# Softmax reciprocals taken on four sums instead of 256 copies of them, and a new hand-ordered issue table

## The chip, the cores and the metric

The kernel runs on one core of one Trainium2 chip. The metric is the device time of one execution in microseconds. Three runs of the kernel before gave 616.99, 620.66 and 622.17 us; their median is 620.66 us. The engines are PE (matrix multiply; PEld is its weight load), DVE (vector), ACT (activations), POOL (GpSimd) and SP, which here only issues DMAs.

## What is computed

Three stages, one behind the other, on 1152 tokens of width 512:

```python
# attention, B=2, H=8, S=576, D=64
scores = q @ k.T / 8 + bias          # bias: a 32-wide MLP of log1p|i-j| / log1p(max(i,1)), per head
attn = exp(scores - max)
attn = attn / (attn.sum(-1) + 1e-9)  # the sums and their reciprocals
x = (attn @ v) as [1152, 512]
# MLP, 512 -> 2048 -> 512
h = x @ w_in;  g = h * tanh(softplus(h));  y = g @ w_out
# mixture of 8 experts, 512 -> 1024 -> 512, one expert per token, at most 288 tokens each
e = argmax(y @ w_gate);  p = softmax(y @ w_gate)[e]
out = p * (relu(y @ w1[e]) @ w2[e])  # rows over the capacity stay zero
```

## The kernel before

**Tiling.** Tokens go in five tiles `it` = 0 to 4 of 256, 256, 256, 256 and 128 rows (the last holds the end of both batches). For each tile the program writes a bias block to memory (`bias_block`, L453) and reads it back by head, does attention head pair by head pair (`pair`, L523; `recips`, L577; `pv_pair`, L598; `x_out`, L615), then the MLP in eight steps (`mlp_a`, L711; `mlp_b`, L738), and writes `y` to the scratch tensor `yscr` and chooses each row's expert (`y_out`, L812; `rank_of`, L881). In the first 160 us the raw weights `wi` and `wo` are also turned into pairs of 16-bit numbers (`conv_row`, L632), with DVE, ACT and POOL sharing the passes over 128x1024 blocks.

**The reciprocals.** For a tile and a head pair the exponentials (L552) leave their row sums in a small tile `rsm`, 128x4 (128x2 in the last tile). `recips` adds 1e-9 (through helper line L279) and takes reciprocals (L588) with an input that reads each sum 64 times, so that one instruction makes a 128x256 tile (128x128 in the last). PE transposes it (L593), ACT or DVE copies it back from PSUM (L596), and `x_out` multiplies the attention output by it (L626, L629). There are 20 of these: 16 wide, 4 half as wide.

**Order.** Nothing is scheduled at run time. `op(...)` collects the operations of the first two stages with estimated times, and `emit` (L232) issues them in the order of a table of numbers, `ORDER`: a number divided by 8 is the operation, and the remainder chooses one of its `alt` forms, that is, the engine. Each engine runs its own queue in that order and waits, at the head of its queue, for what an instruction needs. The estimated times written in the `op` calls and the dependences of an operation that issues nothing change no instruction; only the table does. Which slot of a ring a buffer gets follows from the order too.

**The end of the second stage.** The last tile's `y` (128 rows) goes to `yscr` by two writes of 64 rows (L847, L848). SP's queue also holds the loads of the first expert's weights (`load1`, L1001, and `load2`, L1004, 512 KB each). The choice of experts ends in `gid0` (L991), the row numbers of the first expert's tokens; it needs sums `acc` that L962 adds up on POOL or DVE. Then POOL gathers those rows from `yscr` (L1163), which needs `gid0` and every write to `yscr`. SP reads the table of slots (L1156). The experts (L1176 to L1273) are written in program order, outside the table; four of the eight are run with these inputs.

```python
o.ways[c % 8][2]()          # emit: the chosen form of operation c // 8
gather(0)                   # POOL: three indirect DMAs, xg <- yscr by gid0
```

Of the kernel before, what the change touches and what calls it, by code (L numbers as in the profile page):

```python
# [22 lines left out]
P = 128  # L23
# [239 lines left out]
def tile_kernel(ctx: ExitStack, tc: tile.TileContext, a: dict, cap: int):  # L263
# [313 lines left out]
    def recips(it, ct):  # L577
# [6 lines left out]
        def f():  # L584
            x = sm.t[:, 4:4 + 2 * n]
            ts(dve, x, sm.t[:, 0:2 * n], 1e-9, ALU.add)
            (s0, n0), (s1, _) = x.ap
            dve.reciprocal(wide().rearrange("p (c i r) -> p c i r", c=n, i=2), bass.AP(x.tensor, x.offset, [[s0, n0], [s1, n], [s1 * n, 2], [0, 64]]))  # L588
# [789 lines left out]
```

## Time and profile before

| | before |
|---|---|
| median of three runs | 620.66 us (616.99 to 622.17) |
| profiled execution, its own time | 622.87 us |
| its span, first to last instruction | 621.1 us |
| busy: PE, DVE, ACT, POOL | 513.6, 439.9, 353.9, 129.9 us |
| mean granted TensorE clock | 0.92 of full speed |

The profiled execution's own time is 1.8 us above its span, and 2.2 us above the median. Busy shares are means over stages with different limits: weight conversion and the first attention tiles up to about 160 us, a long middle of attention and MLP up to 480 us, the change to the experts up to 510 us, then the experts. A clock of 1.00 is 2.4 GHz, 0.50 is 1.2 GHz; means between them are mixtures of the two.

### The profile page before, as it was taken

Reading aid. Unit: us, or ns where it says so; the run is one execution under the profiler, and the core shown is the slowest. Engines: PE = TensorE matmul, PEld = TensorE weight load, DVE = VectorE, ACT = ScalarE, POOL = GpSimd, SP = SyncE. Lnnn points to the kernel's source line nnn. Section 1 sums busy time; section 2 is a strip of 40 time slices with the busy share of each in tenths; the row PEclk is TensorE's granted clock in tenths of the full one; section 3 lists DMA queues with packets and bytes.
Section 4 is the critical chain, followed back from the end, with each engine's and each line's share of the span. In section 5 each row is a group of like instructions: output and inputs, shape, how many; then the busy total and the mean of one; then the engine's idle time right before and its main releaser. Section 6 shows DMA issues by size and latency. Waiting matters only on the chain.

```text
span 621.1 us, 11278 instructions
## 1 busy us (share of the span) xinstructions
PE 513.6 (83%) x4212; PEld 356.2 (57%) x4212; DVE 439.9 (71%) x966; ACT 353.9 (57%) x699; POOL 129.9 (21%) x152
## 2 busy tenths in 40 slices
PE   2562787999989989989899988979798539999975
PEld 0110345676567554445676654658556529999963
DVE  6998999899857849777866857346767725546462
ACT  7899888786645856765634653324544204545451
POOL 3502313012001120210011043115114410123212
PEclk9656689799999989999999999979899859999998
DMA  7987566510101225213443010213002245182810
GB/s 305 351 312 265 213 215 221 164 51 1 39 22 54 90 79 173 91 59 134 143 129 94 1 47 0 62 58 120 2 1 69 51 159 203 39 298 57 319 43 27
DMA packets 28468, 73.92 MB, mean 119 GB/s; under 512 B 5126, under 2 KB 5254, under 8 KB 26352
## 3 DMA queue, kind: packets, MB, share of 16 engines
q1 hardware_dynamic: 26704, 68.95, 32.6%
q0 software_dynamic: 1696, 4.11, 2.1%
q8 instruction: 36, 0.59, 0.4%
q14 instruction: 32, 0.26, 0.1%
HBM read 55.67 MB, written 17.61 MB: 118 GB/s over the span
## 4 chain that ended last, share of the span: by engine, by line
PE 52%; DVE 24%; DMA 9%; issue 7%; ACT 4%; POOL 2%; SPq 1%; POOLq 0%; DVEq 0%; ACTq 0%
PE pb L753 10%; PE pb L720 7%; PE pb L612 6%; DMA xg<-yscr,gid 5%; PE ps L720 5%; PE ps L534 4%; DVE rw L282 3%; PE py L1209 3%; PE ph L1186 3%; DVE ra L551 2%; PE pb L560 2%; PE pt L1186 2%; DVE ra L282 2%; DVE ra L588 2%; PE pb L472 2%
## 5 line engine op out<-in xcount | busy, mean ns | idle before, releaser
L720 PEld LDWEIGHTS <-WIt 128*128 128x128 f16 x960 | 86.9, 100 | 23.2 <-issue 12.0
L720 PE MATMUL pb<-PX,WIt 128*128 128x256 f16 (+1 forms) x672 | 74.4, 267 | 1.3 <-DVE ra L282 1.3
L753 PE MATMUL pb<-WOt,ra 128*128 128x512 f16 x276 | 67.4, 390 | 2.1 <-DVE ra L282 2.1
L552 ACT ACTIVATE ra<-ra,rm 128x576 f32<-128x576 f32 x58 | 44.8, 774 | 24.7 <-DVE rm L551 23.2
L460 ACT ACTIVATE ra<-AT,b1c,stab 128x528 f32<-128x528 f32 (+14 forms) x79 | 56.0, 749 | 2.3 <-DVE rm L551 1.3
L472 PE MATMUL pb<-ra,w2s 128*32 128x512 f32 (+17 forms) x248 | 39.3, 620 | 18.8 <-ACT ra L460 8.3
L534 PE MATMUL ps<-AT,rq 64*128 64x512 f32 (+1 forms) x160 | 44.4, 687 | 4.1 <-DVE rm L551 2.9
L753 PEld LDWEIGHTS <-ra 128*128 128x128 f16 x276 | 27.0, 100 | 32.5 <-issue 7.0
L612 PE MATMUL pb<-ra,AT 128*64 128x128 f32 (+1 forms) x660 | 40.7, 273 | 1.6 <-DVE ra L563 1.6
L551 DVE CUSTOM_DVE_ANT_0 ra<-ps,ra 128x576 f32<-128x576 f32 x48 | 34.9, 748 | 8.9 <-PE ps L537 8.7
L1209 PE MATMUL py<-HH,W 128*128 128x288 f32 x288 | 40.4, 298 | 0.0
L1008 DVE TENSOR_TENSOR W<-AT,W 128x1024 fp32r<-128x1024 f32 x28 | 33.7, 1223 | 9.2 <-ACT W L1007 8.4
L279 POOL TENSOR_SCALAR rw<-rw 128x1024 uint32<-128x1024 uint32 (+1 forms) x17 | 23.4, 1377 | 78.0 <-DMA rw<-wo 26.3
L1209 PEld LDWEIGHTS py<-HH,W 128*128 128x128 f32 x288 | 38.8, 188 | 0.0
L720 PE MATMUL ps<-PX,WIt 128*128 128x256 f16 (+1 forms) x288 | 32.5, 266 | 7.6 <-DVE ra L282 3.5
L612 PEld LDWEIGHTS pb<-ra,AT 128*64 128x64 f32 x660 | 34.1, 142 | 6.9 <-issue 4.3
L282 DVE SCALAR_TENSOR_TENSOR rw<-rw 128x1024 int32<-128x1024 int32 (+1 forms) x25 | 32.4, 1295 | 1.1 <-POOL rw L279 1.0
L560 PE MATMUL pb<-ident,ra 128*128 128x128 f32 x183 | 30.2, 290 | 2.2 <-ACT ra L552 1.9
L472 PEld LDWEIGHTS pb<-ra,w2s 128*32 128x32 f32 x248 | 8.1, 128 | 37.4 <-ACT ra L460 16.0
L1007 ACT ACTIVATE W<-AT 128x1024 fp32r<-128x1024 f32 x28 | 29.0, 1054 | 0.0
L537 PEld LDWEIGHTS ps<-AT,rq 128*128 128x128 f32 (+1 forms) x80 | 10.9, 186 | 30.4 <-issue 30.4
L563 ACT COPY ra<-pb 128x384 f32<-128x384 f32 x45 | 20.3, 475 | 13.9 <-PE pb L560 13.9
(386 smaller groups left out, 1114.5 us busy)
## 6 DMA issues: line engine op xcount, KB each, us to landing
AT<-m SPq DMA_DIRECT2D x32, 512.0 KB, 5.3
bscr<-rbe SPq DMA_DIRECT2D x36, 295.5 KB, 3.6
rw<-wo SPq DMA_DIRECT2D x8, 1024.0 KB, 5.3
ra<-bscr SPq DMA_DIRECT2D x24, 288.0 KB, 3.7
WOt<-wi SPq DMA_DIRECT2D x4, 1024.0 KB, 12.5
rw<-wi SPq DMA_DIRECT2D x4, 1024.0 KB, 15.6
AT<-k SPq DMA_DIRECT2D x4, 576.0 KB, 6.6
rw<-bscr SPq DMA_DIRECT2D x8, 288.0 KB, 3.1
```

The costliest lines, as they stand in the source:

```text
L282: (eng or dve).scalar_tensor_tensor(out=out, in0=in0, scalar=s, in1=in1, op0=op0, op1=op1)
L460: on_act = lambda h_=h_, g=g: act.activation(h_.t[:, 0:dn], T[:, 0:dn], AF.Relu, scale=stab[:, g:g + 1], bias=b1c)
L472: pe.matmul(ps.t[32 * c:32 * c + 32, 0:d1 - d0], w2s, hs[c].t[:, d0:d1], start=True, stop=True)
L534: pe.matmul(s_.t[r, 1024 * i:1024 * i + 512], q_.t[hs, c], kraw[hs, k0 + 576 * bb:k0 + 576 * bb + 512], start=True, stop=True)
L551: op("DVE", c_dve(S), lambda i=i, own=own, m_=m_, b_=b_: dve.tensor_tensor_reduce(out=own(), in0=blk(s_.t[:, 960 * i:960 * i + S]), in1=bl ...
L552: op("ACT", c_act(S, 2), lambda i=i, m_=m_, col=col: act.activation(t_.t[:, S * i:S * i + S], t_.t[:, S * i:S * i + S], AF.Exp, bias=m_.t[ ...
L560: pe.transpose(pa.t[:, P * j:P * j + P], t_.t[:, 384 * n + P * j:384 * n + P * j + P], ident)
L612: pe.matmul(ov[64 * i:64 * i + 64, ct % 2, w * bb:w * bb + w], v_, t_.t[:, at + c0:at + c0 + w], start=n == 0, stop=n == 4)
L720: pe.matmul(ps.t[:, n * f_:n * f_ + n], WI[:, wv, ct, P * ft:P * ft + P], xt.t[:, xv, ct, 0:n], start=i == 0, stop=i == 11)
L753: pe.matmul(y_.t, gv()[:, g2, c:c + P], WO[:, wv, ft], **kw)
L1008: dve.tensor_tensor(out=dst[:, 1], in0=src, in1=dst[:, 0].bitcast(F32), op=ALU.subtract)
L1209: pe.matmul(ps[:, 0:SL], W2[:, wv, ft, P * dt:P * dt + P], HH[:, hv, ft], start=ft == 0 and i == 0, stop=ft == 7 and i == 2)
```

## The change

Three things are changed. `recips` takes the reciprocal of the 128x4 sums in place and then copies the four numbers over the 256 columns, as an operation of its own that the table may give to DVE or ACT. Four estimates that the table was made from are different numbers, and the operation that stands for the gather and issues nothing now names `yscr`. And the table itself is new throughout.

```diff
 ORDER = [
-    160, 304, 1192, 120, 136, 168, 144, 152, 192, 312, 112, 176, 200, 1200, 128, 1209, 0, 8, 208, 88, 16, 760, 1216,
...
+    160, 416, 14552, 112, 152, 304, 120, 14560, 312, 168, 136, 144, 176, 200, 128, 1192, 1200, 0, 8, 208, 530, 768,
...
-        op("PE", 1150, f, bytes=0.5, r=[q_, ("k", ct), "kt"], w=[s_], p=["Kfree"], mode=2)
+        op("PE", 1277, f, bytes=0.5, r=[q_, ("k", ct), "kt"], w=[s_], p=["Kfree"], mode=2)
...
-        def f():
-            x = sm.t[:, 4:4 + 2 * n]
-            ts(dve, x, sm.t[:, 0:2 * n], 1e-9, ALU.add)
-            (s0, n0), (s1, _) = x.ap
-            dve.reciprocal(wide().rearrange("p (c i r) -> p c i r", c=n, i=2), bass.AP(x.tensor, x.offset, [[s0, n0], [s1, n], [s1 * n, 2], [0, 64]]))
-        op("DVE", 210 + 133 * n, f, w=[sm, b_], lk=1)
+        x = lambda: sm.t[:, 4:4 + 2 * n]
+
+        def small():
+            ts(dve, x(), sm.t[:, 0:2 * n], 1e-9, ALU.add)
+            dve.reciprocal(x(), x())
+        op("DVE", 210, small, w=[sm])
+
+        def ends_():
+            (s0, n0), (s1, _) = x().ap
+            return wide().rearrange("p (c i r) -> p c i r", c=n, i=2), bass.AP(x().tensor, x().offset, [[s0, n0], [s1, n], [s1 * n, 2], [0, 64]])
+        op("DVE", c_dve(P * n), lambda: dve.tensor_copy(*ends_()), r=[sm], w=[b_], alt=[("ACT", c_act(P * n), lambda: act.copy(*ends_()))])
...
-        op("PE", 1095 if it < NIT else 1300, f, ...
+        op("PE", 1142 if it < NIT else 1300, f, ...
...
-    op("POOL", 3700, lambda: None, r=["gid0"], w=["xg"])
+    op("POOL", 1000, lambda: None, r=["gid0", "yscr"], w=["xg"])
```

In the changed kernel lines behind the table stand one further down, and those behind `recips` six further down (L588 is L589, the new copy is L595, L1163 is L1169).

**SP, end of the second stage.** `AT<-m` are the loads of the first expert's weights, `yscr` the writes of y, `tb` the read of the slot table. Before:

```order
L303 DMA yscr<-rw_110 128x512
L1004 ISA
L1004 DMA AT<-m 128x2x512
L303 DMA out<-ra_112 128x512
L303 DMA yscr<-rw_110 64x512
L1004 ISA
L1004 DMA AT<-m 128x2x512
...
L303 DMA yscr<-rw_110 64x512
L303 DMA yscr<-ra_114 128x512
L1156 ISA
L1156 DMA tb_4581<-tbl 96x3x2
```

Now:

```order
L1010 DMA AT<-m 128x2x512
L304 DMA yscr<-ra_117 128x512
L304 DMA yscr<-ra_114 128x512
L1010 ISA
L1010 DMA AT<-m 128x2x512
L304 DMA yscr<-rw_110 128x512
L304 DMA out<-ra_118 128x512
L304 DMA yscr<-ra_118 64x512 x2
L1162 ISA
L1162 DMA tb_4601<-tbl 96x3x2
```

Before, the first 64 rows of the last tile stand ahead of two weight loads, and the other 64 rows and a block of 128 rows behind them. Now all weight loads stand ahead of the last tile's rows, and the two writes of 64 rows are the last ones, together.

**POOL, the same place.** `tbl` is the scatter into the slot table, `acc` the sums for `gid0`, `xg` the gather. Before:

```order
L915 DMA tbl_81<-pk6_165,rm5_130 2304x2
L962 TENSOR_TENSOR acc1_176<-acc1_176,rw2_110 128x288
L915 DMA tbl_81<-pk7_166,rm0_125 2304x2
L915 DMA tbl_81<-pk8_167,rm9_134 2304x2
L962 TENSOR_TENSOR acc0_175<-acc0_175,ra3_114 128x288
L1163 DMA xg0_4573<-yscr_80,gid0_184 96x512
```

Now:

```order
L921 DMA tbl_81<-pk6_165,rm11_136 2304x2
L921 DMA tbl_81<-pk7_166,rm4_129 2304x2
L921 DMA tbl_81<-pk8_167,rm7_132 2304x2
L968 TENSOR_TENSOR acc1_176<-acc1_176,ra6_117 128x288
L968 TENSOR_TENSOR acc1_176<-acc1_176,rw0_108 128x288
L968 TENSOR_TENSOR acc0_175<-acc0_175,rw1_109 128x288
L1169 DMA xg0_4593<-yscr_80,gid0_184 96x512
```

One addition stood between the last scatter and the gather; now there are three.

**DVE, the second reciprocal of the program before and the first one now** (`rsm` are the sums, `rw`, `WOt` and `WIt` weights under conversion, L551 or L552 the pass over the scores). Before:

```order
L279 TENSOR_SCALAR WOt_106<-rw0_108,sout_100 128x2x512
L551 ISA ra7_118,rm9_134<-ps_140,ra6_117 128x18x32
L551 ISA rm9_134 128x1
L279 TENSOR_SCALAR rsm1_138<-rsm1_138 128x4
L588 RECIPROCAL ra0_111<-rsm1_138 128x256
L282 SCALAR_TENSOR_TENSOR rw1_109<-rw1_109 128x1024
```

Now:

```order
L283 SCALAR_TENSOR_TENSOR rw2_110<-rw2_110 128x1024
L280 TENSOR_SCALAR rsm0_137<-rsm0_137 128x4
L589 RECIPROCAL rsm0_137<-rsm0_137 128x4
L280 TENSOR_SCALAR ra2_113<-AT_104,stab_88,nb1_85 128x352
L595 COPY ra5_116<-rsm0_137 128x256
L280 TENSOR_SCALAR ra9_120<-AT_104,stab_88,nb1_85 128x352
```

The wide reciprocal has become a 128x4 one and a 128x256 copy with another instruction between them. Of the 20 copies the table gives 9 to DVE (8 wide, 1 half) and 11 to ACT (8 wide, 3 half). Counted over the first two stages, DVE also gives up seven of the 128x512 subtractions L735 to POOL, seven PSUM copies L563 and six conversions L734 (four wide) to ACT, and five 128x1024 scaling passes of the weights, most of them DVE's, go to POOL; it takes over two 128x1024 scalings from ACT.

## Rows read from the trace of the kernel before

**Rows 1.** The 40 slices of the span: busy tenths of PE, and the granted clock.
```profile
PE   2562787999989989989899988979798539999975
PEclk9656689799999989999999999979899859999998
```

**Rows 2.** Stretches: length, busy PE, PEld, DVE, ACT, POOL, clock, DMA share, GB/s.
```profile
0.00:80.00 80.00, 38.33 (x192) 11.75 (x192) 71.62 (x125) 69.35 (x127) 23.73 (x50) 0.70 0.77 280
80.00:160.00 80.00, 73.67 (x586) 49.29 (x586) 73.77 (x145) 60.01 (x126) 14.57 (x11) 0.94 0.40 134
160.00:480.00 320.00, 288.88 (x2547) 189.78 (x2546) 219.71 (x525) 170.68 (x356) 61.22 (x64) 0.98 0.22 69
480.00:510.00 30.00, 13.55 (x190) 11.64 (x187) 17.61 (x85) 5.82 (x14) 9.65 (x9) 0.68 0.29 78
```

**Rows 3.** Groups by line: engine, operation, shapes, count | busy us, mean ns.
```profile
L588 DVE RECIPROCAL ra<-rsm 128x256 f32<-128x256 f32 x10 | 17.5, 1753 | 0.4
L588 DVE RECIPROCAL ra<-rsm 128x128 f32<-128x128 f32 x4 | 3.8, 953 | 0.1
L876 DVE RECIPROCAL pk<-rr 128x1 f32<-128x1 f32 x9 | 1.5, 164 | 0.3
L596 DVE COPY ra<-pb 128x256 f32<-128x256 f32 x2 | 0.8, 419 | 0.0
L596 ACT COPY ra<-pb 128x256 f32<-128x256 f32 x6 | 2.3, 385 | 3.8 <-PE pb L593 3.8
L552 ACT ACTIVATE ra<-ra,rm 128x576 f32<-128x576 f32 x58 | 44.8, 774 | 24.7 <-DVE rm L551 23.2 <-DVE fl L1012 1.2
```

**Rows 4.** Chain that ended last, in order of time: first and last of ten reciprocals.
```profile
78.59 1.76 DVE ra L588
...
360.06 1.75 DVE ra L588
```

**Rows 5.** Timeline of DVE: the last of the six reciprocals that start before 160 us.
```profile
145.06 1.75 DVE L588 RECIPROCAL ra<-rsm 128x256 f32<-128x256 f32 x1
```

**Rows 6.** Who waited for the instructions of L588: us, times.
```profile
  PE pb L593: 3.8, 2
  PE ps L593: 2.8, 3
```

**Rows 7.** Chain that ended last, from the last matmul of stage two to the gather.
```profile
481.37 5.39 PE pb L757 x96
...
491.58 0.59 ACT rw L846
492.23 0.47 SPq L303
...
494.49 6.84 DMA yscr<-ra
...
502.54 0.94 POOL xg L1163
```

**Rows 8.** DMA issues: destination and source, queue, count, KB each, us to landing.
```profile
yscr<-rw SPq DMA_DIRECT2D x6, 256.0 KB, 3.3
```

**Rows 9.** Timeline of DVE and POOL at that place: start us, us, instruction.
```profile
479.56 0.73 POOL L962 TENSOR_TENSOR acc<-acc,rw 128x288 f16<-128x288 f16 x1
...
493.93 1.83 POOL L962 TENSOR_TENSOR acc<-acc,ra 128x288 f16<-128x288 f16 x1
493.97 1.21 DVE L1041 TENSOR_TENSOR W<-AT,W 128x1024 fp32r<-128x1024 f32 x1
...
496.92 0.16 DVE L991 TENSOR_TENSOR gid<-pb,smsk 96x3 uint32<-96x3 f32 x1
```

**Rows 10.** Timeline of PE: a wait and what it is followed by.
```profile
414.11 2.72 PE L720 MATMUL ps<-PX,WIt 128*128 128x256 f16 x12 [3.15 <-DVE rr L279]
...
419.18 1.47 PE L720 MATMUL ps<-PX,WIt 128*128 128x256 f16 x12
```

**Rows 11.** The stretch of PE behind that wait; columns as in rows 2.
```profile
414.00:419.00 5.00, 4.89 (x24) 3.45 (x24) 2.06 (x3) 0.00 (x0) 1.04 (x1) 0.50 0.00 0
```

More of the change, by code (lines that the diff above doesn't have):

```diff
@@ L612, in f @@
                         pe.matmul(ov[64 * i:64 * i + 64, ct % 2, w * bb:w * bb + w], v_, t_.t[:, at + c0:at + c0 + w], start=n == 0, stop=n == 4)
-        op("PE", 1095 if it < NIT else 1300, f, bytes=0.5, r=[("tT", it, ct, b, n) for n in range(3)] + [("v", ct), ("v", 4)], p=[o_, "Vfree"], hold=[t_], mode=1)
+        op("PE", 1142 if it < NIT else 1300, f, bytes=0.5, r=[("tT", it, ct, b, n) for n in range(3)] + [("v", ct), ("v", 4)], p=[o_, "Vfree"], hold=[t_], mode=1)
     def x_out(it, ct):
```

199 rows, old and new, of the table ORDER are left out of this document.

## The prediction

> **What bounds the kernel now.** I first cut the span into slices and stretches. Until 160 us DVE is the fullest engine: 71.6 of the first 80 us and 73.8 of the next 80 [rows 2], converting weights between passes over scores. PE is loaded from 80 us on and has 80 - 73.7 = 6.3 us free there. From 160 to 480 us PE is the bound: 288.9 of 320 us, 31.1 us idle, DVE only 219.7 [rows 2]. Between 480 and 510 us no engine is full, and the slices show PE at 5 and 3 tenths with a lower clock there [rows 1]. Behind it the experts run as a program of their own, which the change does not touch.
>
> Then I followed the chain that ended last. Ten of the twenty reciprocals stand on it, with 1.75 us each [rows 4]. Direct waits at the transposes behind reciprocals are smaller, 3.8 + 2.8 us on PE [rows 6]. At the end of the second stage the chain reads: last matmuls of y, the copy of the last rows on ACT (over at 492.17), its write from SP at 492.23, then a write of other rows that is issued only at 494.49 and takes 6.84 us to land at 501.33, then the gather at 502.54 [rows 7]. It waits for a transfer, not for work: a write of 256 KB usually lands in 3.3 us [rows 8], and this one stands in the queue behind two loads of 512 KB. The row numbers for the gather had been ready at 496.92 + 0.16 = 497.08 [rows 9].
>
> **The small reciprocal.** A wide one takes 1753 ns, a half one 953 [rows 3]. That is 800 / 128 = 6.25 ns a column and 153 ns besides, so four columns are about 178 ns, and two 165; the 128x1 reciprocals take 164 [rows 3]. DVE saves 16 x 1.575 + 4 x 0.788 = 28.4 us. The new copy from SBUF to SBUF isn't in the trace. Its nearest rows are the copies of the same width from PSUM, 0.419 us on DVE and 0.385 on ACT [rows 3]; I bound it below by the shortest DVE row, 0.164, and above by the 0.774 of a pass over 576 columns [rows 3], and take 0.42 and 0.385, the same width. Nine copies on DVE cost 3.6 us, so DVE is relieved by 24.7 us; ACT gets 3.9 us more and has 20 of 80 us free even in its fuller stretch from 80 us [rows 2].
>
> *Before 160 us* six of the wide ones start, at 78.6 to 145.1 us [rows 4, 5]. They save 6 x 1.575 = 9.5 us; four of their six copies go to DVE (1.7 us), so 7.8 us are left on the engine that sets the pace. PE's work there stays the same, and its 6.3 us of idle time are the ceiling. I take 5, between nothing and 6.3, near the ceiling because nothing else is full.
>
> *After 160 us* seven of the chain's ten reciprocals stand (three are among the six). Each can give at most 1.75 - 0.18 - 0.42 = 1.15 us, together 8. But PE is 90% busy there, and a reciprocal that ends a wait has a neighbour that ends it next: the accumulation behind it, or a pass over scores. I take half, 4, between nothing and 8.
>
> **The table.** Beyond the reciprocals DVE hands over twenty other passes, some 12 us in all, to ACT and POOL. Most lie in the middle stretch, where DVE has 100 us free. They are slower on POOL but off the pace-setting engine. The order of the loads in the first 80 us differs too, with the same bytes. What a new order does to PE's 31.1 us of idle time cannot be read from the trace of before: it may give back half, 15 us, or lose as much by waits like the one at 414 us. I take 0 as the likeliest, and keep both ends for the rivals.
>
> **The last rows of y.** Now all weight loads stand ahead of the last tile's rows, behind the writes of earlier tiles alone. The two last writes go out together from 492.2 us. With 3.3 us to land, for half the bytes each, `yscr` is complete at about 492.7 + 3.3 = 496.0, and what comes next in line is the row numbers. These now wait for three additions on POOL in place of one. Behind the last scatter, which ended at 493.93, three times 0.73 us end at 496.1; the one addition ended at 495.76 [rows 9]. So `gid0` moves from 497.1 to about 497.5, and the gather, with the same 502.54 - 501.33 = 1.2 us behind its last input, to 498.7: 3.8 us earlier, said as 4. The write of the slot table is queued ahead of the additions on POOL, as before, and the DVE passes of L1041, one of which stood ahead of `gid0` for 1.21 us [rows 9], now all stand earlier. SP's read of the slot table and the second expert's loads follow at once and move along.
>
> One addition took 1.83 us, beside a DVE pass of 1.21 us that began with it, and another 0.73 alone [rows 9]. Three at 1.83 would end at 499.4, `gid0` would come at 500.7, and the gather would gain only 0.6 us. The Trainium skill ("SBUF — State Buffer", section "Who interferes with whom") says that a DVE instruction with two SBUF inputs and a GpSimd instruction that reads SBUF hold each other off for a whole instruction; the trace agrees, 1.10 us more beside 1.21. By that rule the additions would cost 0.73 here, as no such long DVE pass stands beside them any more, while the subtractions now given to POOL would collide more often.
>
> **Sum.** 5 + 4 + 0 + 4 = 13 us, from the profiled execution's own 622.87 to 609.9. That execution is 2.2 us above the median of the three runs, so I expect a median of 607.7, said as **608 us**, 2% under 620.66. Within 1%, 614.5 to 626.9, is about what a measurement of this kernel cannot tell from no change.
>
> **Rivals** (all as medians, 2.2 us under the sum from 622.87):
>
> *PE is the bound and takes it all back*, chance 0.17. For it: PE at 92% from 80 us and 90% from 160 us [rows 2]; against it, ten reciprocals on the chain. Only the 4 us at the end stay: 616.7.
>
> *The additions on POOL take the place of the late write*, chance 0.10. For it the 1.83 us; against it that the long DVE pass has gone. 5 + 4 + 0.6 = 9.6 in all: 611.1. By the rule of the Trainium skill named above ("SBUF — State Buffer", "Who interferes with whom") this needs a long DVE pass beside each of the three.
>
> *The new table is much the better one*, chance 0.15. DVE's 37 us less leave PE fewer waits, half of its 31.1 us goes: 5 + 15 + 4 = 24, so 596.7. For it: each stall costs twice, see below. Against it: a new order can add waits as well as remove them.
>
> *ACT's queue holds up PE*, slower, chance 0.08. Eleven transposes of PE now wait for a copy that stands in ACT's queue behind exponentials of 0.774 us and PSUM copies. Where PE reaches its transpose with four of these ahead, it stands 4 x 0.774 = 3.1 us. A stand of 3.15 us cost more than itself: the next group of twelve matmuls, and another like it, ran in 2.72 us, not 1.47 [rows 10], 2.5 us more, at a granted clock of 0.50, which is 1.2 GHz [rows 11]. So 5.7 us each; three in eleven are 17 us, against 9 kept: 622.87 + 8 - 2.2 = 628.7. Under an average of some 1.2 us per ACT copy it is still no loss. ACT's 47% idle time in the middle [rows 2] speaks against it.
>
> The forecast itself, 602 to 614, gets 0.50. That gives 0.75 for faster by over 1% (forecast, additions, better table), 0.17 for within 1%, and 0.08 for slower. The range that holds eight in ten goes from 597, the middle of the better table, to 618, past the case in which PE takes it all back.
>
> **What would show it.** In the profile after: 128x4 reciprocals of about 0.18 us and copies near 0.4; DVE's total busy time down by 30 to 37 us; in the stretch to 160 us the first MLP matmuls some 5 us earlier; the chain with no reciprocal on it; the write of `yscr` gone from the chain before the gather, and the gather 3 to 5 us sooner after the last copy of y. Wrong would be: PE waits at L594 to L600 for ACT copies, added waits of over 3 us with groups at half clock, POOL additions at 1.8 us ending last, or a first stretch as long as before because loads come later.

## The result: 4.6% faster, more than twice the forecast gain

The changed kernel took 590.94 us (median of four runs, 588.77 to 594.74) against 619.6 us; the ratio is 0.9544, 95% interval 0.9479 to 0.961. That is 28.3 us of 620.7 (the median of the 23 runs of before that the first experiments were set beside), where 12.7 were forecast; the time lies under the range that was given. The profiled execution took 590.54 us in a span of 588.8, at a mean clock of 0.947. In the new kernel's line numbers L593 and L596 are L599 and L602, L720, L753 and L757 are L726, L759 and L763, and L962 and L991 are L968 and L997. The experiments add lines of their own at the top, so theirs differ again by some lines; tile names and shapes stay. Here `pb` and `ps` are banks of PSUM, the memory in which PE leaves its results until other engines have read them.

The slices of the profile after, as [rows 1] of before:

```profile
PE   1655788998979788999999999999899379999975
PEclk9876799999999998999999999999999669999998
```

The same stretches as [rows 2], and one more, of the last third (length, then busy PE, PEld, DVE, ACT, POOL, then clock, DMA share, GB/s):

```profile
0.00:80.00 80.00, 44.56 (x266) 18.40 (x266) 72.65 (x141) 72.10 (x131) 29.60 (x54) 0.81 0.85 304
80.00:160.00 80.00, 71.47 (x574) 47.59 (x567) 71.31 (x149) 58.54 (x126) 23.07 (x16) 0.98 0.33 110
160.00:480.00 320.00, 288.37 (x2687) 195.22 (x2686) 208.31 (x581) 176.67 (x383) 75.10 (x73) 0.97 0.25 77
340.00:460.00 120.00, 113.94 (x1212) 81.59 (x1204) 84.15 (x224) 58.98 (x127) 33.45 (x32) 1.00 0.17 57
```

PE's idle time in the first 80 us fell from 41.7 to 35.4 us and its clock rose from 0.70 to 0.81. From 340 to 460 us PE is 95% busy at the full clock. The third line looks like that of before only because it now reaches into the change to the experts, whose first matmul starts at 477.4 us.

The groups that answer to [rows 3] (busy us, mean ns, idle before):

```profile
L602 ACT COPY ra<-pb 128x256 f32<-128x256 f32 x8 | 3.1, 383 | 1.3 <-PE pb L599 1.2
L589 DVE RECIPROCAL rsm<-rsm 128x4 f32<-128x4 f32 x16 | 2.8, 178 | 0.5
L595 ACT COPY ra<-rsm 128x256 f32<-128x256 f32 x6 | 2.5, 414 | 3.7 <-DVE rsm L589 3.7
L595 DVE COPY ra<-rsm 128x256 f32<-128x256 f32 x6 | 2.3, 383 | 0.1
```

The reciprocal takes the 178 ns that were worked out, and the wide copies of these rows 383 ns on DVE and 414 on ACT where 420 and 385 were taken. DVE's busy time is 409.5 us, 30.4 less.

The end of stage two. First the chain, as [rows 7]:

```profile
464.78 3.28 DMA tbl<-pk,rm
468.10 0.89 PE pb L991 x9
...
470.37 0.94 POOL xg L1169
```

Then the timelines of SP, POOL and DVE there, as [rows 9]:

```profile
463.30 1.14 SPq L304 DMA_DIRECT2D yscr<-ra  x2
...
465.82 0.74 POOL L968 TENSOR_TENSOR acc<-acc,ra 128x288 f16<-128x288 f16 x1
466.64 1.41 POOL L968 TENSOR_TENSOR acc<-acc,rw 128x288 f16<-128x288 f16 x2
...
469.21 0.16 DVE L997 TENSOR_TENSOR gid<-pb,smsk 96x3 uint32<-96x3 f32 x1
```

No write of `yscr` stands ahead of the gather any more. The row numbers do: the three additions end at 468.05, `gid0` at 469.37, and the gather begins 1.0 us behind it. The chain puts PE's matmuls of L991 at 468.10 down to the last scatter, which landed at that moment too; that they need the additions and not the scatter shows in T1 below, where they start 1.1 us after the scatter was issued, with the additions done.

Where the time went shows best by work done. The table gives the start, in us, of the first-MLP matmul groups (80 groups of twelve) and of the first expert matmul, counted in the traces; S0 is an experiment below, all of the change but the new table.

| | before | S0 | after |
|---|---|---|---|
| group 1 | 126.9 | 120.5 | 116.4 |
| group 17 | 190.5 | 183.3 | 181.9 |
| group 49 | 393.5 | 381.6 | 381.5 |
| group 61 | 428.8 | 415.7 | 404.4 |
| group 77 | 451.6 | 438.7 | 426.0 |
| first expert matmul | 509.5 | 492.6 | 477.4 |

Each column is one execution. In S0 and after, PE has done the same matmuls when groups 17 and 61 begin. At group 49 it has not: the new order has then done 71 more matmuls of other kinds, so that row does not compare like with like. After leads S0 by 4.1 us at group 1, 1.4 at group 17, 11.3 at group 61, 12.7 at group 77 and 15.2 at the first expert matmul. The start alone differs from execution to execution by some us: five executions that begin with the old order and the small reciprocal (E1, K2, S0, H1 and H4 below) start group 1 at 118.5, 118.8, 120.5, 121.4 and 122.4 us, two with the old order and the wide one (before, and E3 below) at 126.9 and 124.3.

### The profile page after: what moved, and what is told of

It reads as the page before. It is cut to its first block, busy times and chain, and to the rows that moved or that the text cites. A ratio compares the mean times of both kernels' runs of the same rounds, so it can differ in the third digit from the quotient of the medians.

```text
span 588.8 us, 11288 instructions
## 1 busy us (share of the span) xinstructions
PE 501.7 (85%) x4212; PEld 353.1 (60%) x4212; DVE 409.5 (70%) x957; ACT 355.5 (60%) x718; POOL 148.8 (25%) x162
## 4 chain that ended last, share of the span: by engine, by line
PE 44%; DVE 22%; issue 15%; DMA 7%; ACT 7%; POOL 3%; SPq 0%; POOLq 0%; DVEq 0%; ACTq 0%
PE pb L759 9%; PE pb L726 8%; DMA xg<-yscr,gid 5%; PE ps L726 4%; PE ps L535 4%; PE pb L618 4%; DVE rw L283 4%; PE pb L561 3%; DVE ra L552 2%; DVE ra L280 2%; PE ps L561 2%; DVE WOt L283 2%; DMA w2b<-w 2%; PE ps L538 2%; PE pb L763 2%
## 5 line engine op out<-in xcount | busy, mean ns | idle before, releaser
L726 PEld LDWEIGHTS <-WIt 128*128 128x128 f16 x960 | 85.2, 98 | 25.9 <-issue 11.2
L726 PE MATMUL pb<-PX,WIt 128*128 128x256 f16 (+1 forms) x648 | 71.5, 265 | 2.7 <-DVE ra L283 2.0
L461 ACT ACTIVATE ra<-AT,b1c,stab 128x384 f32<-128x384 f32 (+13 forms) x74 | 51.8, 740 | 5.3 <-PE ps L473 2.2
L759 PE MATMUL pb<-WOt,ra 128*128 128x512 f16 x228 | 54.3, 383 | 0.2 <-POOL ra L741 0.2
L473 PE MATMUL pb<-ra,w2s 128*32 128x512 f32 (+15 forms) x246 | 39.5, 612 | 16.5 <-DVE rbe L490 5.3
L280 POOL TENSOR_SCALAR rw<-rw 128x1024 uint32<-128x1024 uint32 (+1 forms) x19 | 28.6, 1507 | 59.4 <-DMA rw<-wo 23.3
L552 DVE CUSTOM_DVE_ANT_0 ra<-ps,ra 128x576 f32<-128x576 f32 x50 | 36.4, 753 | 8.4 <-PE ps L538 3.9
L726 PE MATMUL ps<-PX,WIt 128*128 128x256 f16 (+1 forms) x312 | 31.7, 256 | 9.2 <-ACT ra L461 3.1
L759 PE MATMUL pb<-WOt,rw 128*128 128x512 f16 x156 | 38.3, 387 | 0.0
L618 PE MATMUL pb<-ra,AT 128*64 128x128 f32 (+1 forms) x620 | 35.8, 266 | 0.9 <-DVE ra L632 0.9
L759 PEld LDWEIGHTS <-ra 128*128 128x128 f16 x228 | 21.8, 98 | 24.1 <-issue 1.5
L618 PEld LDWEIGHTS pb<-ra,AT 128*64 128x64 f32 x620 | 30.6, 137 | 5.1 <-issue 2.5
L473 PEld LDWEIGHTS pb<-ra,w2s 128*32 128x32 f32 x246 | 10.1, 128 | 33.0 <-issue 8.6
```

The costliest lines, as they stand in the source:

```text
L280: eng.tensor_scalar(out=out, in0=in0, scalar1=s1, scalar2=s2, op0=op0, op1=op1)
L461: on_act = lambda h_=h_, g=g: act.activation(h_.t[:, 0:dn], T[:, 0:dn], AF.Relu, scale=stab[:, g:g + 1], bias=b1c)
L473: pe.matmul(ps.t[32 * c:32 * c + 32, 0:d1 - d0], w2s, hs[c].t[:, d0:d1], start=True, stop=True)
L552: op("DVE", c_dve(S), lambda i=i, own=own, m_=m_, b_=b_: dve.tensor_tensor_reduce(out=own(), in0=blk(s_.t[:, 960 * i:960 * i + S]), in1=bl ...
L618: pe.matmul(ov[64 * i:64 * i + 64, ct % 2, w * bb:w * bb + w], v_, t_.t[:, at + c0:at + c0 + w], start=n == 0, stop=n == 4)
L726: pe.matmul(ps.t[:, n * f_:n * f_ + n], WI[:, wv, ct, P * ft:P * ft + P], xt.t[:, xv, ct, 0:n], start=i == 0, stop=i == 11)
```

## The experiments

All ratios are to runs of the kernel before on the same chip; us are (1 - ratio) x 620.7.

**Reciprocals and order, each alone.** E1: the old table, with the reciprocal taken on the sums.

```diff
-            dve.reciprocal(wide().rearrange("p (c i r) -> p c i r", c=n, i=2), bass.AP(x.tensor, x.offset, [[s0, n0], [s1, n], [s1 * n, 2], [0, 64]]))
+            dve.reciprocal(x, x)
+            dve.tensor_copy(wide().rearrange("p (c i r) -> p c i r", c=n, i=2), bass.AP(x.tensor, x.offset, [[s0, n0], [s1, n], [s1 * n, 2], [0, 64]]))
```

> The table of before, unchanged; only the reciprocal is taken on the sums and then copied over the columns, both on DVE and in the place of the wide one. Theory A (the forecast's prices were right and the table gave the rest): the 5 and 4 us of the two terms, so about 611 us, ratio 0.985. Theory B (the reciprocals were underpriced, since each stands on the chain and each wait of PE is followed by matmuls at half clock): 20 us or more, 600 us or less, ratio 0.968 or less. Nothing (617 or more) would say that PE takes it all back.

Measured: 607.96 us, ratio 0.9811 (0.9754 to 0.9869), 11.7 us gained, 8.1 to 15.3 by the interval. Theory A, with its 9 us inside the interval; B is out. PE's second stretch in E1, and then in S0 and E3 below, which have the same order there, S0 with the small reciprocal and E3 with the wide one (columns as above):

```profile
80.00:160.00 80.00, 76.32 (x630) 50.29 (x626) 73.98 (x166) 65.18 (x138) 16.60 (x13) 1.00 0.38 134
80.00:160.00 80.00, 76.58 (x620) 50.13 (x620) 72.17 (x162) 64.35 (x135) 17.34 (x13) 0.97 0.40 134
80.00:160.00 80.00, 74.68 (x600) 49.52 (x599) 74.61 (x149) 61.73 (x128) 16.66 (x13) 0.96 0.40 134
```

Before, it was 73.67 us at clock 0.94 [rows 2]. With the small reciprocal PE is busy for 1.6 to 2.9 us more of this stretch. Its clock there is 0.96 to 1.00 in the five executions named under the table, against 0.94 and 0.96; how much of that the reciprocal gave is not shown. The first MLP matmul starts at 120.3 us on the mean of the five and at 125.6 on the mean of the two, 5.3 us earlier; E1's own 118.5 against 126.9 pairs the earliest with the latest. From group 17 to group 61 E1 takes 230.8 us and S0 232.4, before 238.3 and E3 237.1: another 6.1 us.

E2: the new table, with the wide reciprocal.

```diff
-            dve.reciprocal(x(), x())
...
-        op("DVE", c_dve(P * n), lambda: dve.tensor_copy(*ends_()), r=[sm], w=[b_], alt=[("ACT", c_act(P * n), lambda: act.copy(*ends_()))])
+        op("DVE", c_dve(P * n), lambda: dve.reciprocal(*ends_()), r=[sm], w=[b_], alt=[("DVE", c_dve(P * n), lambda: dve.reciprocal(*ends_()))])
```

> The new table, with the reciprocal taken wide again on DVE in the place of the copy. Theory A: the 9 us come back, about 600 us, and the table with the tail keeps some 20 us of the gain. Theory B: 610 us or more, since the table then has little of its own. If the table took DVE off PE's way so far that the reciprocals no longer matter, it stays within 3 us of 591.

Measured: 599.12 us, ratio 0.965 (0.9594 to 0.9706), 6.6 us less gain than the whole change. Theory A again: under the new table the small reciprocal is worth 6.6 us and under the old one 11.7, each good to some 4 or 5 us, and the rest is the table's.

**The last rows of y.** E3: the old table with three entries moved, two loads of the first expert and the late write of 256 KB.

```diff
+for c in (12112, 14312, 14288):
+    ORDER.remove(c)
+at = ORDER.index(14304) + 1
+ORDER[at:at] = [12112, 14312, 14288]
```

> The table of before, with the last two bulk loads and the late write of 256 KB put ahead of the last rows of y. The forecast's term: about 4 us, 616 us, ratio 0.9935; the gather is then released by the row numbers, some 1.2 us behind 497.1 us of the profile of before in place of 502.5. Rival: another transfer ends last in its place, under 1 us, ratio above 0.998.

Measured: 616.87 us, ratio 0.9939 (0.9906 to 0.9972), 3.8 us gained, 1.7 to 5.8 by the interval. In its trace the last rows' writes are issued from 488.98 us, `gid0` ends at 494.09, and the gather begins 1.0 us later, as in the profile after. The write is gone from the end.

**All but the table.** S0 puts E1 and E3 together. All its copies stay on DVE, right behind the reciprocals.

> The old table with the small reciprocal and with the last rows of y behind the bulk loads: all of the change but the new order. If the parts add up: 608 less 3.8 = 604 us, ratio 0.975, and the new order itself is worth 13 us. If the tail is worth nothing once the reciprocals are short, 608; if the order's 13 us need it, 600 or less.

Measured: 606.18 us, ratio 0.9743 (0.9686 to 0.9799), 16.0 us gained against 11.7 + 3.8 = 15.5: the parts add up. So the new table (its order, its engines, and its 11 copies on ACT), without the tail, is worth 0.9743 - 0.9544 = 0.0199, 12.4 us, or 7 to 18 by the two intervals. That is the term which the forecast put at 0.

**Where the order gains.** Four kernels have the first part of one table and the rest of the other, with the small reciprocal in all. A few entries (two in H1, none in H2, three each in H3 and H4) stand some places later than in their table, since no buffer would have been free for them, and two operations of H3 have another form. In short, with the old table numbered as the new kernel is:

```diff
-ORDER = NEW
+ORDER = OLD[:1350] + [c for c in NEW if c // 8 not in {d // 8 for d in OLD[:1350]}]
```

H1 is this; H2 has the tables exchanged; H3 cuts at 450 and H4 at 1500.

> The small reciprocal; the first 1,350 operations (to about 337 us in both profiles) in the order and on the engines of the old table, the remaining 476 by the new one, the tail with them. The old table throughout gave 608, the new one 591. Theory late (the new table's own gain lies behind 337 us, where the old order leaves PE two waits of over 3 us with half clock behind each, at 398 and 425 us, and the tail): 592 us, 594 at most. Theory early (it lies in the loads and in the first tiles): only the tail's 4 us, 604.

> The reverse: the first 1,350 operations by the new table, the rest by the old one, with the old tail. Theory late: 606 us or more. Theory early: 595, which is 591 and the tail's 4 us.

> The old table for the first 450 operations (to about 118 us: the loads, the bias, the first scores), then the new one. The first matmuls over scores start 7 us earlier under the new table. If that lead is worth its 7 us at the end: 598 us. If it is only work done in another order and is lost before 180 us: 594 us or less.

> The old table for the first 1,500 operations (to about 390 us), then the new one for the last 326. If the two waits at 398 and 425 us (3.15 and 3.48 us, each with about 2.5 us more at half clock behind it: some 11 us) and the tail (4 us) are the whole of it: 592 to 594 us. If what is done early decides whether they come: 600 or more.

Measured: H1 596.52 us, ratio 0.959 (0.9519 to 0.9661); H2 611.06, 0.9841 (0.9785 to 0.9897). Behind operation 1350 the new table and its tail are worth 0.0221 (13.7 us) after an old beginning (E1 to H1), and 0.0297 (18.4 us) after a new one (H2 to the whole change). Each cut joins two orders that were not made for each other, so a part of both losses may be the cut's own. H1's 596.52 lies 2.5 us above the bound of theory late and 7.5 below that of theory early, H2 is where theory late put it: the gain lies late. H3 with 606.5 us (0.9765, 0.971 to 0.9821) and H4 with 610.64 (0.9817, 0.9737 to 0.9897) met neither number. H3 is slower than H1, which has more of the old table, so its loss can't be that of the old loads; a cut in a busy place seems to cost by itself, and these two say nothing on the lead of 7 us at the start. In H4 the groups 61 to 77, just behind its cut, take 31.3 us, where S0 has 23.0 and after 21.6, so H4's loss too is in part the cut's. What the last 326 entries are worth alone stays open.

The stretches from 160 to 340 us in S0 and after, and then the one from 340 to 460 us in S0:

```profile
160.00:340.00 180.00, 169.53 (x1429) 108.47 (x1428) 125.66 (x335) 110.60 (x228) 20.80 (x21) 0.99 0.29 92
160.00:340.00 180.00, 166.17 (x1421) 106.92 (x1419) 114.64 (x307) 115.33 (x250) 34.75 (x33) 0.99 0.30 93
340.00:460.00 120.00, 106.35 (x982) 73.00 (x981) 69.14 (x177) 53.43 (x112) 35.98 (x37) 0.96 0.14 42
```

From 160 to 340 us the new table fills PE no better. From 340 to 460 us PE is idle for 13.65 us in S0 and loses up to 0.04 x 120 = 4.8 to the clock; after, it is 6.06 and none. That is some 12 us, as much as the table is worth. What PE waited for in S0 from 340 to 462 us (us in all, times, longest):

```profile
PE ps L727 <- DVE ra L288: 3.5, 1, 3.5
PE ps L727 <- DVE rr L285: 3.2, 1, 3.2
PE pb L760 <- DVE ra L288: 1.8, 1, 1.8
```

And the timeline of PE in S0 at the two longest:

```profile
402.15 2.72 PE L727 MATMUL ps<-PX,WIt 128*128 128x256 f16 x12 [3.15 <-DVE rr L285]
404.67 1.65 PE L727 MATMUL pb<-PX,WIt 128*128 128x256 f16 x12
...
429.36 1.44 PE L727 MATMUL ps<-PX,WIt 128*128 128x128 f16 x12 [3.48 <-DVE ra L288]
```

The first is the wait of [rows 10], 12 us earlier and still 3.15 us: the reciprocals did not touch it. By the code, DVE's pass in each is the last that reads a PSUM bank which PE's next matmuls want. In the profile after, the same view has no wait over 1.3 us:

```profile
PE ps L726 <- DVE rw L283: 2.0, 2, 1.3
PE pb L907 <- DVE o L280: 1.1, 1, 1.1
PE ps L726 <- ACT ra L731: 0.8, 1, 0.8
```

**Order, or which engine does what.** E4 keeps the new order and gives all 252 operations that changed engine or form their old ones; K1 does so for 62 behind operation 1350, three of which are new copies that go from ACT to DVE; K2 has the old order of S0 with the new engines for the other 59.

```diff
+WAYS = {
...
+}
+ORDER = [c // 8 * 8 + WAYS.get(c // 8, c % 8) for c in ORDER]
```

> The new table's order and the small reciprocal, but each of the 252 operations whose engine or form the new table changed is put back on the engine that it had before (the new copies stay as they are). Theory C (what the table gives lies in which engine does what): more than half of some 16 us comes back, 599 us or more. Theory D (it lies in the order): 594 us or less. An order made for other engines may also lose more than both, above 607, and then it tells neither.

> The new table; of the operations behind the 1,350th (337 us) the 62 that changed engine or form are put back where they were, among them 26 multiplications and subtractions of the MLP between POOL and DVE. Theory engines (what the new table wins behind 337 us is won by which engine does what): 599 us or more. Theory order (it is won by what follows what on PE): 594 or less.

> The reverse of that: the old order with the small reciprocal and the tail, and behind 337 us the engines of the new table. Theory engines: 604 less at least half of 13, 597 or less. Theory order: 601 or more.

Measured: E4 622.95 us, ratio 1.0036 (1.0003 to 1.007), 0.4% slower than the kernel before, which by its own expectation tells neither. K1 603.91, 0.9728 (0.9678 to 0.9777): all that the order gave is gone. K2 606.87, 0.9792 (0.9738 to 0.9845): no gain over S0. K1 is what theory engines asked for and K2 what theory order asked for, so neither holds alone. Behind 337 us the new engines are worth nothing in the old order, and the new order nothing with the old engines.

**Which of the 62.** K3 puts back six multiplications of the MLP (POOL in place of DVE), K4 the other 56, K7 of these 56 the thirteen conversions to 16 bit and thirteen subtractions, K8 the remaining thirty, the three new copies among them. All have the new order; K3 is shown, the others have longer lists.

```diff
+WAYS = {1161: 0, 1431: 0, 1444: 0, 1483: 0, 1714: 0, 1774: 0}
+ORDER = [c // 8 * 8 + WAYS.get(c // 8, c % 8) for c in ORDER]
```

> The new table, in which six of the MLP's multiplications behind 337 us go back from DVE to POOL. One takes 1.29 us on POOL and 0.69 to 1.05 on DVE in the profile of the new table, and the pass on DVE that reads PSUM for the last time, and so gives PE the bank back, stands right behind it. Theory banks (PE's waits in the last third are for banks, and these six give them back late): more than half of the 13 us come back, 598 us or more. Otherwise 594 or less.

> The counterpart: these six stay on DVE, and the other 56 operations behind 337 us go back to their old engines, thirteen subtractions and thirteen conversions of the MLP, eight copies of transposes and others. Theory banks: 595 us or less. If these carry it, 599 or more. Some of both would give 594 to 600 in each of the two runs.

> The new table, in which of the 56 only the thirteen conversions to 16 bit and the thirteen subtractions behind them go back to their old engines (eight conversions from ACT to DVE, eight subtractions from POOL to DVE, five of each the other way). All 56 cost some 10 us. Theory MLP chain (DVE, with these passes back ahead of the ones that free a PSUM bank, holds up PE's next MLP matmuls): at least 5 of the 10, 596 us or more. If the copies and additions carry it: 593 or less.

> The counterpart, the other thirty of the 56: copies of transposes, of y and of the PSUM sums, splits of x and the four additions ahead of the row numbers. Theory MLP chain: 595 us or less, of which 1 to 2 us for the additions and the last copies of y, since PE waited 5.44 us for the last addition where all 56 were back, against 4.29. Otherwise 597 or more.

| | time, us | ratio (interval) | of the gain given back, us |
|---|---|---|---|
| K3 | 590.92 | 0.9524 (0.9473 to 0.9575) | none |
| K4 | 601.33 | 0.969 (0.9639 to 0.9742) | 9.1 |
| K7 | 598.59 | 0.9671 (0.9606 to 0.9735) | 7.9 |
| K8 | 596.69 | 0.9604 (0.9554 to 0.9654) | 3.7 |

My theory that the multiplications carry it fell: six on the slower engine cost nothing. The conversions and subtractions cost the most, and more than their expectation asked for. DVE in K7, ahead of the pass that PE waits for:

```profile
426.76 0.41 DVE L746 CAST rw<-ra 128x512 f16<-128x512 f32 x1
427.20 0.69 DVE L747 TENSOR_TENSOR rw<-ra,rw 128x512 f16<-128x512 f32 x1
427.81 0.48 DVE L289 SCALAR_TENSOR_TENSOR rw<-rw,gsc,ps 128x256 f32<-128x256 f32 x1
```

PE's next matmuls start at 428.35, after 2.09 us of waiting for that third instruction. In the profile after, ACT and POOL have those two passes, and the wait there is 1.30 us. K7's row first, then that of after:

```profile
428.35 2.85 PE L732 MATMUL ps<-PX,WIt 128*128 128x128 f16 x48 [2.09 <-DVE rw L289]
426.02 2.85 PE L726 MATMUL ps<-PX,WIt 128*128 128x128 f16 x48 [1.30 <-DVE rw L283]
```

That is the mechanism which K7's expectation names, but for 0.8 us of the 7.9. Two more waits in K7 are for subtractions themselves (L747), ahead of the second MLP's matmuls; after has 0.2 us of that kind (window 380 to 485 us):

```profile
PE pb L769 <- DVE rw L747: 1.2, 1, 1.2
PE pb L765 <- DVE ra L747: 0.8, 1, 0.8
```

Together these are 2.6 us; what made up the rest is not shown. K8's 596.69 us lies between the two numbers of its expectation, and its 3.7 us are not clear of the noise, as the intervals of K8 and the whole change overlap by half.

**Going on from the new table.** T1 has the last three additions on DVE (its edit is shown); K6 has the seven late multiplications that are still on POOL there, by the same two lines with other numbers.

```diff
+WAYS = {1215: 1, 1548: 1, 1550: 1}
+ORDER = [c // 8 * 8 + WAYS.get(c // 8, c % 8) for c in ORDER]
```

> The new table with the last three additions ahead of the row numbers on DVE in place of POOL. In the profile of the new table they end at 468.05 us on POOL, three of 0.73, and PE waits 4.29 us for them. On DVE, where each can follow its own mask, they end at some 465.5, and the last rows of y, written from 463.3 us, land next, at about 467.7 by the 3.3 us of such a write: the gather comes 1 to 2 us sooner, about 589 us. If another transfer (the slot table's) is what the gather waits for, nothing: within 0.5 us of 591.

> The new table, in which the last seven multiplications behind 337 us that are on POOL go to DVE as well. PE is busy 113.9 of the 120 us from 340 to 460 us there, so at most some 3 us can come: 588 to 591 us by theory banks. DVE is busy 84 of these 120 us and gets some 5 more; if it then holds up the score passes or the last tile, it is 593 or more.

Measured: T1 592.21 us, 0.9527 (0.9488 to 0.9566); K6 591.41, 0.9525 (0.9477 to 0.9573). Neither can be told from the whole change; no version that ran beats it by more than the noise. In T1's timelines the additions are short and the gather is late for another reason:

```profile
466.54 0.98 POOL L925 DMA_INDIRECT tbl<-pk,rm  x1 [3.58 <-DVE rm L284]
466.75 0.30 DVE L972 TENSOR_TENSOR acc<-acc,ra 128x288 f16<-128x288 f16 x1
467.09 0.53 DVE L972 TENSOR_TENSOR acc<-acc,rw 128x288 f16<-128x288 f16 x2
...
468.77 0.16 DVE L1001 TENSOR_TENSOR gid<-pb,smsk 96x3 uint32<-96x3 f32 x1
...
470.83 0.94 POOL L1173 DMA_INDIRECT xg<-yscr,gid  x1 [3.31 <-DVE v L1134]
```

The gather begins 1.9 us behind the end of `gid0` where it was 1.0. It was not the writes of `yscr`: they are issued from 465.56 us, and the last, issued at 466.10, landed 2.4 us later, ahead of `gid0`. The last scatter into the slot table is left, the case that the expectation allowed for: in POOL's queue a wait ahead of the gather ends at 469.78, 3.24 us after the scatter was issued, and in E3 and K8, whose traces hold the landing of that scatter, the same wait ends 0.03 us behind it. T1's own trace does not hold that landing. From group 77 on the gather comes after 42.9 us, where it was 44.4, so the 1 to 2 us are there; the experts then took 114.4 us against 111.4, which the edit does not touch.

## Why the prediction was wrong

**The step that failed** is the table: "I take 0 as the likeliest". It is worth 12.4 us (S0 to the whole change). The terms 5, 4 and 4 came out as 11.7 for the first two together (E1) and 3.8 (E3). Of the 15.6 us that the forecast lacks, 12.4 are this term's and 2.7 those of the first two, nearly all of it behind 160 us.

*Before 160 us, 5.* Right: 5.3 us by the means of five executions against two. The ceiling was worked out too low, though it was not passed: I named PE's 6.3 us of idle time as the most that could come back, but the row beside it [rows 2] shows the clock at 0.94, up to 0.06 x 80 = 4.8 us more.

*After 160 us, 4.* Too small: E1 and S0 gain 6.1 us between groups 17 and 61, so the half that I took of 8 was nearer to three quarters. The working counts ten reciprocals at 1.75 us on the chain of before; one of them stands there for 1.17 only.

*The small reciprocal.* 178 ns each, as worked out. The copies cost nearly what was taken. The sign that I gave, a chain with no reciprocal on it, did not come: seven still stand on the chain of after, but with 0.19 us or less each. ACT's queue held up no transpose for long: at L599 PE waited 1.7 us in all, 0.9 at most, and none of it for a copy of L595 on ACT. The rival on it is out.

*The table, 0.* I argued that what an order does cannot be read from the trace of before. Whether this order would cure the waits could indeed not be read. But where there was something to cure could, had I cut the long stretch in two. In the trace of before:

```profile
340.00:460.00 120.00, 105.72 (x1016) 74.45 (x1013) 72.84 (x172) 53.64 (x111) 30.07 (x31) 0.96 0.12 38
```

14.3 us idle and up to 4.8 lost to the clock in 120 us, with DVE at 61%, ACT at 45% and POOL at 25%: PE loses up to 16% while nothing else is full, so its waits come from what stands ahead of what in the queues, and on which engine. The rival on a much better table put 15 us on this, for the right reason ("each stall costs twice"), but spread over the whole middle and with a chance of 0.15. The gain is in the last third, as the stretches up to and from 340 us show, and H1 and H2 with them.

*What I said of DVE's relief* fell as well. Behind 337 us not the amount handed over matters (with the old order, K2, it is worth nothing), but which passes go: conversions and subtractions were worth 7.9 us (K7), in part because they no longer stand ahead of the pass that frees PE's bank.

*The last rows of y, 4.* Right in size and in mechanism: E3 gained 3.8; the additions took 0.74 and twice 0.7 where three times 0.73 were taken, and the gather came 1.0 us behind `gid0` where 1.2 were. The rival in which the additions take 1.83 each is out. DVE ran no pass with two SBUF inputs beside them, so by the rule of the Trainium skill ("SBUF — State Buffer", "Who interferes with whom") they had nothing to wait for, and the trace agrees.

## What to carry to other kernels

When you put a ceiling on what can come back in a stretch, count the clock's loss beside the idle time; from 340 to 460 us the change gave back both. Cut a long stretch until the part in which the bounding engine loses most stands alone; where no other engine is full there, a new order has something to win, and 0 is a poor guess for it. Try an order and its choice of engines together: here neither was worth anything without the other. Before you read a gain from one trace against one other, look at how far executions of the same instructions lie apart.

## What the runs showed of the hardware

A pass that is cheap on DVE can become long beside POOL. In the profile after, the 128x512 `TENSOR_SCALAR` of L280, whose median is 0.43 us where POOL ran no two-input pass, took 2.13 us where two of them ran beside it, one behind the other (DVE and POOL timelines):

```profile
422.46 2.13 DVE L280 TENSOR_SCALAR ra<-rw 128x512 f32<-128x512 f32 x1 [0.57 <-ACT rw L731]
...
422.47 1.16 POOL L741 TENSOR_TENSOR ra<-ra,ra 128x512 f16<-128x512 f32 x1
423.58 0.73 POOL L736 TENSOR_TENSOR rw<-rw,ra 128x256 f32<-128x256 f32 x1
```

It ended just behind the second, at 424.59 against 424.31. Four more such passes met a two-input pass of POOL; they took 0.54, 0.54, 0.75 and 1.38 us. The Trainium skill ("SBUF — State Buffer", "Who interferes with whom") says that such a pass can enter a mode in which it needs the port pair that GpSimd uses, and that whoever comes second is blocked for the whole instruction; the trace agrees that the DVE pass stood for two POOL instructions in a row, but not that it came second, as both started within 0.01 us, DVE first. The PE wait of 1.30 us at 426.02 stands behind this one. So the subtractions that the new table gave to POOL are not free, and still, with the conversions, a gain of 7.9 us.

The same instructions can run at another mean clock in another execution. From the first expert matmul on, where no edit changes anything, E4's profiled execution and T1's are:

```profile
508.70:618.00 109.30, 99.04 (x704) 93.57 (x704) 57.70 (x90) 48.12 (x79) 21.05 (x19) 0.97 0.45 150
477.80:592.20 114.40, 102.57 (x704) 95.99 (x704) 57.79 (x90) 48.22 (x79) 21.37 (x19) 0.93 0.42 143
```

The same 704 matmuls took 5.1 us more at 0.93 than at 0.97. Differences of a few us between two single traces are therefore no finding by themselves.
